# Fused attention, convolution and experts: counts summed in PSUM, the last tile in halves, three instead of five convolution units on TensorE, and new order tables

## The chip, the cores and the metric

The kernel runs on one core of a Trainium2 chip. Its time is device microseconds (us) per execution. Engines are named as in the profile: PE is TensorE's matmul side and PEld its weight loads, DVE is VectorE, ACT is ScalarE, POOL is GpSimd, and SP is SyncE, which here issues most DMAs. Lnnn is a line of the kernel before.

## What is computed

Attention on 8 batches of 8 heads, 256 tokens, 64 columns a head; a gated depthwise convolution of 15 taps over the tokens; and a mixture of 16 experts in which every token goes to one expert. All data are float32.

```python
attn = softmax(q @ k.T / 8)                       # per batch and head
x = (attn @ v)  -> (batch, token, 512)
xg = x * sigmoid(glu_gate)
conv[s, d] = sum_k pad(xg)[s + k, d] * conv_w[d, k]   # 15 taps, 7 zeros at each end
x = x + silu(conv)                                # 2048 tokens of 512 columns
g = argmax(x @ w_group);  e = argmax(x @ w_expert[g])
out = p(g) * p(e) * (relu(x @ w1[g, e]) @ w2[g, e])   # w1 512x1024, w2 1024x512
```

## The kernel before

**Tiling.** Work is cut into 16 units. A unit is one block of 128 channels (two heads) of two batches; four units, one for each channel block, make a group, so that group g holds batches 2g and 2g+1. Tiles lie with channels on the partitions and tokens along the free dimension, so most instructions work on 128x512 elements (two batches of 256 tokens).

**A unit.** `pair` (L472) makes the scores of two heads (L490), `head` takes their maximum on DVE (L519), the exponentials on ACT (L524) and transposes them on PE (L531); the transposes go back to SBUF as `pT`, and the product with v is L510. `tail` (L545) spreads the reciprocal sums into `rb`, transposes them on PE (L568), copies them out of PSUM (L570), multiplies (L577 to L582) and makes the gated `xg` (L586 to L593). A site such as `rb` or `xg` may run on one of two or three engines. Plain copies and casts go through one helper, and the trace shows them all at its line, L293.

**The convolution.** In `conv` (L640) DVE runs one multiply-add for each tap (L669, L671) into a PSUM bank. A few first taps may instead be made by ACT (L660) and added on POOL (L663). In `conv_pe` (L608) SP first copies `xg` four times, each partition in four shifted versions, into four weight buffers (L616); then PE multiplies them with small diagonal matrices, 16 matmuls of 32 rows by 512 columns (L626). Which units go this way stands in `PC`; 1 to 3 belong to group 0, and 4 and 5 to group 1. Then come tanh, the silu product (L636 or L691), the sum with x (L703), and the split of x into a rounded part `xh` and a rest `xl`.

**Routing.** Once four units of a group are done, `route` (L751) makes the logits on PE (L763), then a chain of small DVE instructions from L787 to L854 with three short visits to PE (L771, L819, L840/L841). For every batch of 256 tokens the expert that most of them chose is picked (L824, L826), and SP reads its number and fetches its weights (L860, L865). The place of every other token in its expert's list needs sums of one-hot counts over earlier tiles; `cum`, made by L836 and L838, is their running sum over the four tiles of a group.

**Experts.** A weight tile of 128x1024 arrives in `raw`, is rounded into `wh` (L884), and the rest is `wl` = raw - wh (L888, two halves). `dense` multiplies all 256 tokens of a batch with the chosen expert, three products for each pair of rounded and rest parts: 96 matmuls up (L914), then 48 of 512 columns down (L935 to L937) into two banks, one for each tile of 128 tokens. `store` (L966) scales a tile by the token's weight and sends it out. Tokens with another expert are gathered in lists of 32 (L1103 to L1201) and scattered over the result; a loop at the end takes what is left.

**The order.** Every engine runs its instructions in the order in which the program issues them. `Flow` makes that order while the program is built: each step has an engine, an assumed length and a key, and the ready step with the lowest key goes next. `KEYS` shifts the key of a site, `WAYS` picks the engine of each use of a site by a string of digits, `CD` delays the DVE convolution of a group behind other work, and `NSL`, `HB`, `NRAW`, `NPT` and `NPR` are numbers of buffers; `CSC`, `CS0`, `CAC` and `CMO` limit how many PSUM banks scores, convolutions and experts may hold. None of this runs on the chip: only the order and the choice of engines are left in the program.

Of the kernel before, what the change touches and what calls it, by code (L numbers as in the profile page):

```python
# [285 lines left out]
def attn_conv_moe(ctx, tc, aQ, aG, cw, wr, wE, cst, out):  # L286
# [185 lines left out]
    def pair(u, i):  # L472
# [13 lines left out]
        yield at("score", 0, u.k + 0.1 * i, ("PE", 0.875))  # L486
# [58 lines left out]
    def tail(u):  # L545
# [10 lines left out]
        e = yield at("rb", u.n, u.k, ("ACT", 0.1 + 0.21 * nb), ("DVE", 0.07 + 0.14 * nb), ("POOL", 0.5 * nb))  # L556
# [51 lines left out]
    def conv_pe(u):  # L608
# [4 lines left out]
        yield run("SP", 2.4, -20)  # L613
# [85 lines left out]
    def residual(u, acc, ia):  # L699
# [51 lines left out]
    def route(G_):  # L751
# [604 lines left out]
```

## Time and profile before

| | us |
|---|---|
| median of 3 runs | 369.69 |
| lowest and highest | 369.40, 369.95 |
| the profiled execution | 370.42 |
| its span, first to last instruction | 368.6 |
| PE busy | 348.4 (95% of the span) |
| DVE busy | 280.8 (76%) |
| POOL busy | 266.2 (72%) |
| ACT busy | 232.2 (63%) |

The span leaves out 1.8 us of the profiled execution. The shares are means over a kernel with several stages: attention with DMA and softmax in the first 100 us, attention beside experts until about 230 us, and experts alone after that. A matmul is drawn until its modelled end, so that rows of PE overlap; the time that PE needs for a run of matmuls is read from the start of its first to the start of what follows.

### The profile page before, as it was taken

Reading aid. Unit: us, or ns where it says so; the run is one execution under the profiler, and the core shown is the slowest. Engines: PE = TensorE matmul, PEld = TensorE weight load, DVE = VectorE, ACT = ScalarE, POOL = GpSimd, SP = SyncE. Lnnn points to the kernel's source line nnn. Section 1 sums busy time; section 2 is a strip of 40 time slices with the busy share of each in tenths; the row PEclk is TensorE's granted clock in tenths of the full one; section 3 lists DMA queues with packets and bytes.
Section 4 is the critical chain, followed back from the end, with each engine's and each line's share of the span. In section 5 each row is a group of like instructions: output and inputs, shape, how many; then the busy total and the mean of one; then the engine's idle time right before and its main releaser. Section 6 shows DMA issues by size and latency. Waiting matters only on the chain.

```text
span 368.6 us, 7954 instructions
## 1 busy us (share of the span) xinstructions
PE 348.4 (95%) x2766; PEld 277.0 (75%) x2766; DVE 280.8 (76%) x557; ACT 232.2 (63%) x534; POOL 266.2 (72%) x264
## 2 busy tenths in 40 slices
PE   7999999989999996998999999799999999999993
PEld 6666357635798776977787788779988977998982
DVE  3899948895999999999999999999999647201100
ACT  3987678746998653557989887344556534555521
POOL 1664766355887773569995866798869996999891
PEclk9999999999999998999999999899999999999999
DMA  7737964899266452549534332548999965855401
GB/s 269 246 117 177 305 225 150 198 322 325 97 238 218 166 195 77 203 132 339 217 115 172 116 114 88 199 136 288 412 409 390 371 249 186 307 195 181 163 2 64
DMA packets 29084, 77.13 MB, mean 209 GB/s; under 512 B 2999, under 2 KB 3255, under 8 KB 29041
## 3 DMA queue, kind: packets, MB, share of 16 engines
q1 hardware_dynamic: 27008, 72.94, 57.6%
q10 hardware_dynamic: 1872, 3.41, 2.5%
q8 instruction: 24, 0.39, 0.4%
q0 software_dynamic: 160, 0.23, 0.2%
q14 instruction: 20, 0.16, 0.1%
HBM read 63.67 MB, written 7.54 MB: 193 GB/s over the span
## 4 chain that ended last, share of the span: by engine, by line
PE 53%; DVE 25%; ACT 8%; DMA 6%; issue 4%; SPq 1%; POOL 1%; DVEq 0%; ACTq 0%; POOLq 0%
PE bk L914 19%; DVE bk L671 7%; PE bk L935 5%; PE bk L937 5%; PE bk L936 5%; ACT pr L524 5%; DVE nm L519 3%; PE bk L490 3%; PE bk L531 3%; PE bk L510 3%; DVE wl L888 3%; DMA gv<-wE 3%; PE bk L626 2%; DMA gv<-aG 2%; DMA wl<-sl 2%
## 5 line engine op out<-in xcount | busy, mean ns | idle before, releaser
L888 POOL TENSOR_TENSOR wl<-raw,wh 128x512 fp32r<-128x512 f32 x113 | 145.3, 1311 | 12.4 <-ACT wh L293 11.6
L671 DVE SCALAR_TENSOR_TENSOR bk<-sl,cwq,bk 128x512 f32<-128x512 f32 x143 | 102.6, 747 | 1.3
L914 PE MATMUL bk<-sl,wh 128*128 128x256 f32 x512 | 79.2, 294 | 0.0
L293 ACT CAST wh<-raw 128x1024 fp32r<-128x1024 f32 x57 | 60.1, 1054 | 23.9 <-PE bk L937 11.7
L914 PEld LDWEIGHTS bk<-sl,wh 128*128 128x128 f32 x512 | 68.5, 195 | 5.3 <-issue 3.9
L524 ACT ACTIVATE pr<-bk,nm 128x256 f32<-128x256 f32 x128 | 59.4, 493 | 19.4 <-DVE nm L519 18.9
L935 PE MATMUL bk<-wh,hh 128*128 128x512 f32 x128 | 51.8, 405 | 0.0
L936 PE MATMUL bk<-wl,hh 128*128 128x512 f32 x128 | 50.6, 395 | 0.0
L937 PE MATMUL bk<-wh,hl 128*128 128x512 f32 x128 | 50.6, 395 | 0.0
L519 DVE TENSOR_REDUCE nm<-bk 128x2 f32<-128x512 f32 x64 | 40.1, 681 | 8.3 <-PE bk L490 8.2
L961 POOL TENSOR_TENSOR hl<-tm,hh 128x512 fp32r<-128x512 f32 x20 | 27.0, 1352 | 19.8 <-ACT tm L954 14.8
L914 PE MATMUL bk<-sl,wl 128*128 128x256 f32 x256 | 41.4, 285 | 0.0
L531 PE MATMUL bk<-c_id,pr 128*128 128x128 f32 x256 | 36.2, 278 | 4.1 <-ACT pr L524 4.0
L948 ACT ACTIVATE hh<-bk 128x512 fp32r<-128x512 f32 x32 | 19.3, 603 | 31.7 <-PE bk L914 21.8
L531 PEld LDWEIGHTS bk<-c_id,pr 128*128 128x128 f32 x256 | 28.2, 140 | 13.1 <-ACT pr L524 8.3
L914 PEld LDWEIGHTS bk<-sl,wl 128*128 128x128 f32 x256 | 35.6, 193 | 0.0
L490 PE MATMUL bk<-qk 64*128 64x256 f32 x256 | 32.9, 392 | 0.1
L510 PE MATMUL bk<-pT,gv 128*64 128x256 f32 x256 | 32.7, 388 | 0.0
L490 PEld LDWEIGHTS bk<-qk 64*128 64x128 f32 x256 | 23.4, 186 | 7.4 <-issue 4.4
L524 ACT ACTIVATION_READ_ACCUMULATOR pr<-bk,nm 128x1 f32 x128 | 28.8, 225 | 0.0
L935 PEld LDWEIGHTS bk<-wh,hh 128*128 128x128 f32 x128 | 24.1, 188 | 5.9 <-issue 0.8
L937 PEld LDWEIGHTS bk<-wh,hl 128*128 128x128 f32 x128 | 24.1, 188 | 5.8
(161 smaller groups left out, 550.5 us busy)
## 6 DMA issues: line engine op xcount, KB each, us to landing
raw<-wE SPq DMA_DIRECT2D x64, 512.0 KB, 4.5
gv<-wE SPq DMA_DIRECT2D x24, 512.0 KB, 10.0
gv<-aG SPq DMA_DIRECT2D x16, 512.0 KB, 5.7
qk<-aQ SPq DMA_DIRECT2D x15, 512.0 KB, 3.7
wh<-sl SPq DMA_DIRECT2D x10, 270.0 KB, 6.1
wl<-sl SPq DMA_DIRECT2D x10, 270.0 KB, 5.7
out_dram<-y SPq DMA_DIRECT2D x9, 256.0 KB, 4.4
out_dram<-y ACTq DMA_DIRECT2D x7, 256.0 KB, 3.0
```

Source lines behind the costliest of these rows:

```text
L293: (a_.copy if e == "ACT" else on[e].tensor_copy)(o, i)
L490: t_.matmul(scs[hh][:, qt, :], t[sl, i, qt * P:(qt + 1) * P], t[sl, i, 256:512], start=True, stop=True)
L510: t_.matmul(u.a[64 * hh:64 * hh + 64, i, :], u.vt[:, i, kt, hh, :], pTs[hh][1][:, kt, :], start=kt == 0, stop=kt == 1)
L519: v_.reduce_max(nm[:, hh, :], sc, axis=AX.X, negate=True)
L524: a_.activation(pr[:, qt, :], sc[:, qt, :], AF.Exp, bias=nm[:, hh, qt:qt + 1], scale=1.0, accum_out=u.sm[:, i, qt, hh, 0:1])
L531: t_.transpose(tp[:, kt, qt * P:(qt + 1) * P], pr[:, qt, kt * P:(kt + 1) * P], ident)
L671: v_.scalar_tensor_tensor(acc if k == KT - 1 else ac, x, w, acc if k == m and m > 1 else ac, ALU.mult, ALU.add)
L888: on[e].tensor_tensor(wl[:, sl], raw[:, sl], wh[:, sl].bitcast(F32), ALU.subtract)
L914: t_.matmul(hp[:, f, :], ww[:, f, c, :], x, start=k == 0, stop=k == 11)
L935: t_.matmul(ys[t], hh[:, k, sl], w3h[:, k, :], start=j == 0 and k == 0, stop=False)
L936: t_.matmul(ys[t], hh[:, k, sl], w3l[:, k, :], start=False, stop=False)
L937: t_.matmul(ys[t], hl[:, k, sl], w3h[:, k, :], start=False, stop=j == 3 and k == 1)
```

## The change

Four things change.

1. The running sums of the one-hot counts are built in PSUM and copied to SBUF once, instead of being built in SBUF.
2. Of the last batch's second tile, the down product is made as two halves of 256 columns in two banks, each scaled and sent as soon as it is done (`half`), one by DVE and SP, one by ACT.
3. `PC` is 1 to 3: units 4 and 5 take the DVE convolution.
4. All tables are new, with the numbers of buffers, the limits of banks and some assumed lengths, so that sites move between engines and the order differs from about the tenth microsecond on.

```diff
-NSL = 22
-HB = 3
+NSL = 19
+HB = 4
-NRAW = 5
+NRAW = 6
-CD = 598.26, 74.86, 138.82, 696.08
+CD = 653.75, 89.0, 427.88, 891.21
-CSC = 6
-CS0 = 4
-CAC = 5
-CMO = 7
+CSC = 4
+CS0 = 5
+CAC = 3
+CMO = 4
-PC = 1, 2, 3, 4, 5
+PC = 1, 2, 3
...
         cum = small.tile([P, TT, NE], F32, name="cum")
-        v_.tensor_copy(cum[:, 0], ohl[:, 0])
+        sums = ps(0, TT, NE)
+        v_.tensor_copy(sums[:, 0], ohl[:, 0])
         for u in range(1, TT):
-            v_.tensor_tensor(cum[:, u], cum[:, u - 1], ohl[:, u], ALU.add)
-        yield run("PE", 0.5)
+            v_.tensor_tensor(sums[:, u], sums[:, u - 1], ohl[:, u], ALU.add)
+        v_.tensor_copy(cum, sums)
+        yield run("PE", 0.42)
...
-            iy = yield take("bk", 2, "mo", CMO + 2 * (att[0] == NU))
+            iy = yield take("bk", 3 if m.b == B - 1 else 2, "mo", CMO + 2 * (att[0] == NU))
...
+                    if m.b == B - 1 and t == 1:
...
+                        for h in range(2):
+                            yield run("PE", 0.71)
+                            c, yp = slice(h * S, h * S + S), ys[1 + h][:, 0:S]
+                            for k in range(2):
+                                t_.matmul(yp, hh[:, k, sl], w3h[:, k, c], start=j == 0 and k == 0, stop=False)
+                                t_.matmul(yp, hh[:, k, sl], w3l[:, k, c], start=False, stop=False)
+                                t_.matmul(yp, hl[:, k, sl], w3h[:, k, c], start=False, stop=j == 3 and k == 1)
+                            if j == 3:
+                                fl.go(half(m, h, c, y, yp), -5, fl.now[2], "PE")
+                        continue
...
+    def half(m, h, c, y, yp):
+        yield flag(gr[m.g].done)
+        tt = 2 * m.b + 1
+        yield run(("DVE", "ACT")[h], (0.35, 0.33)[h])
+        if h:
+            a_.activation(y[:, c], yp, AF.Copy, scale=rec[:, tt, 1:2])
+        else:
+            v_.tensor_scalar(y[:, c], yp, rec[:, tt, 1:2], None, ALU.mult)
+        w = ("SP", "ACT")[h]
+        yield run(w, 0.43)
+        on[w].dma_start(out=out[tt * P:(tt + 1) * P, c], in_=y[:, c])
```

What the tables make of the program, as numbers of instructions before and after. On DVE: multiply-adds of the convolution (L669, L671) 159 and 179; `wl` halves 15 and 2; copies of `rb` from PSUM 10 and 1; copies of `pT` 20 and 13; casts of `wh` 7 and 4; gated products L593 3 and 7; in all 586 and 580. On ACT: 434 and 462, among them taps of the convolution (L660) 6 and 16, `rb` from PSUM 6 and 15 and `pT` 44 and 51. On POOL: 280 and 290, among them `wl` halves 113 and 126, sums of taps (L663) 0 and 5, and `xg` products (L591) 13 and 9. On SP: copies for `conv_pe` (L616) 20 and 12.

On SP, before, just behind the first three weight fetches of group 0 (L865): `sl_632` is the `xg` of unit 5, `qk` and `gv` are the inputs of later units.

```order
49 L865 DMA raw<-wE 128x1024
50 L616 DMA wh<-sl_632 128x1x540
51 L616 DMA wl<-sl_632 128x1x540
52 L616 DMA wh<-sl_632 128x1x540
53 L616 DMA wl<-sl_632 128x1x540
54 L413 DMA qk<-aQ 128x2x512
55 L747 DMA x_rows<-y 128x512
56 L418 DMA gv<-aG 128x2x512
57 L865 ISA
58 L865 DMA raw<-wE 128x1024
```

The same place now (L867 is L865 of before):

```order
41 L867 DMA raw<-wE 128x1024
42 L413 DMA qk<-aQ 128x2x512
43 L418 DMA gv<-aG 128x2x512
44 L867 ISA
45 L867 DMA raw<-wE 128x1024
46 L867 ISA
47 L867 DMA raw<-wE 128x1024
48 L747 DMA x_rows<-y 128x512
49 L867 ISA
50 L867 DMA raw<-wE 128x1024
```

The four copies are gone, and the inputs of the next unit follow the first weight fetch.

On DVE, before, just ahead of the routing of group 0 (L787 is its first instruction): maxima, copies and a product.

```order
76 L293 COPY y<-bk_809 128x512
77 L593 SCALAR_TENSOR_TENSOR sl_503<-gv,sl_794 128x2x256
78 L554 TENSOR_REDUCE dn<-sm 128x8
79 L555 RECIPROCAL dn<-dn 128x8
80 L293 CAST sl_813<-sl_575 128x2x256
81 L714 TENSOR_TENSOR sl_884<-sl_575,sl_813 128x2x256
82 L293 COPY pT<-bk_800 128x512
83 L787 TENSOR_REDUCE gmx<-bk_809 128x4
```

The same place now, where `sl_553` is the `xg` of unit 4:

```order
73 L671 SCALAR_TENSOR_TENSOR bk_747<-sl_553,cwq,bk_747 128x512 x5
74 L636 SCALAR_TENSOR_TENSOR acc<-sl_441,bk_672 128x512
75 L671 SCALAR_TENSOR_TENSOR bk_747<-sl_553,cwq,bk_747 128x512 x2
76 L519 TENSOR_REDUCE nm<-bk_875 128x2
77 L519 TENSOR_REDUCE nm<-bk_876 128x2
78 L671 SCALAR_TENSOR_TENSOR bk_747<-sl_553,cwq,bk_747 128x512 x3
79 L671 SCALAR_TENSOR_TENSOR acc<-sl_553,cwq,bk_747 128x512
80 L787 TENSOR_REDUCE gmx<-bk_891 128x4
```

The convolution of unit 4, which PE did before, stands on DVE ahead of the routing of group 0.

On PE, before, at the routing of group 1: logits (L763), transposes of its rows (L741), and up products (L914) of the batches of group 0.

```order
509 L763 MATMUL bk_1767<-sl_1248,wr_sb 32x512
510 L741 MATMUL bk_1768<-c_id,sl_1248 128x128
511 L741 MATMUL bk_1768<-c_id,sl_1148 128x128
512 L741 MATMUL bk_1768<-c_id,sl_954 128x128
513 L741 MATMUL bk_1768<-c_id,sl_794 128x128
514 L771 MATMUL bk_1767<-c_sb,y 128x20 x4
515 L741 MATMUL bk_1769<-c_id,sl_1248 128x128
516 L741 MATMUL bk_1769<-c_id,sl_1148 128x128
517 L741 MATMUL bk_1769<-c_id,sl_954 128x128
518 L741 MATMUL bk_1769<-c_id,sl_794 128x128
519 L914 MATMUL bk_1839<-sl_727,wh 128x256
520 L914 MATMUL bk_1839<-sl_669,wh 128x256
```

The same place now (L951 to L953 are L935 to L937 of before):

```order
559 L763 MATMUL bk_1917<-sl_1240,wr_sb 32x512
560 L741 MATMUL bk_1919<-c_id,sl_1240 128x128
561 L741 MATMUL bk_1919<-c_id,sl_1124 128x128
562 L741 MATMUL bk_1919<-c_id,sl_935 128x128
563 L741 MATMUL bk_1919<-c_id,sl_698 128x128
564 L510 MATMUL bk_1940<-pT,gv 64x256 x4
565 L771 MATMUL bk_1917<-c_sb,y 128x20 x4
566 L741 MATMUL bk_1921<-c_id,sl_1240 128x128
567 L741 MATMUL bk_1921<-c_id,sl_1124 128x128
568 L741 MATMUL bk_1921<-c_id,sl_935 128x128
569 L741 MATMUL bk_1921<-c_id,sl_698 128x128
570 L510 MATMUL bk_1940<-pT,gv 64x256 x4
```

Between the short products of the routing PE now has attention and down products; 192 up matmuls stand ahead of this place, where 120 stood before.

## Rows read from the trace of the kernel before

**Rows 1.** The page: span, busy time by engine, shares of the last chain.
```profile
span 368.6 us, 7954 instructions
PE 348.4 (95%) x2766; PEld 277.0 (75%) x2766; DVE 280.8 (76%) x557; ACT 232.2 (63%) x534; POOL 266.2 (72%) x264
PE 53%; DVE 25%; ACT 8%; DMA 6%; issue 4%; SPq 1%; POOL 1%; DVEq 0%; ACTq 0%; POOLq 0%
```
**Rows 2.** Windows: stretch, length, busy by engine, clock, DMA share, GB/s.
```profile
50.00:100.00 50.00, 47.76 (x376) 29.82 (x374) 38.51 (x90) 37.13 (x107) 29.09 (x33) 1.00 0.67 214
100.00:134.90 34.90, 34.90 (x244) 28.76 (x240) 34.47 (x54) 27.14 (x64) 27.17 (x27) 1.00 0.59 211
134.90:231.00 96.10, 91.14 (x649) 76.23 (x648) 93.33 (x180) 68.93 (x164) 69.42 (x67) 0.98 0.46 156
296.70:368.60 71.90, 65.09 (x458) 56.91 (x448) 17.36 (x60) 30.21 (x41) 57.63 (x47) 0.99 0.47 162
```
**Rows 3.** Timeline of PE, 71 to 93 us: start, length, instruction, [idle before].
```profile
71.95 0.62 PE L626 MATMUL bk<-wh,wd 128*32 128x512 f32 x1
...
75.52 1.09 PE L531 MATMUL bk<-c_id,pr 128*128 128x128 f32 x8
...
80.65 1.04 PE L626 MATMUL bk<-wh,wd 128*32 128x512 f32 x2 [1.26 <-DMA wh<-sl]
...
86.98 2.00 PE L490 MATMUL bk<-qk 64*128 64x256 f32 x16
```
**Rows 4.** Timeline of the SP queue, 62 to 82 us.
```profile
76.38 1.68 SPq L616 DMA_DIRECT2D wl<-sl  x1
```
**Rows 5.** Groups by line and form: count | busy, mean ns | idle before.
```profile
L888 POOL TENSOR_TENSOR wl<-raw,wh 128x512 fp32r<-128x512 f32 x113 | 145.3, 1311 | 12.4 <-ACT wh L293 11.6 <-DVE wh L293 0.8
L888 DVE TENSOR_TENSOR wl<-raw,wh 128x512 fp32r<-128x512 f32 x15 | 15.8, 1083 | 0.5 <-ACT wh L293 0.3
L671 DVE SCALAR_TENSOR_TENSOR bk<-sl,cwq,bk 128x512 f32<-128x512 f32 x143 | 102.6, 747 | 1.3
L836 DVE COPY cum<-ohl_all 128x16 f32<-128x16 f32 x4 | 3.0, 754 | 0.1
L838 DVE TENSOR_TENSOR cum<-cum,ohl_all 128x16 f32<-128x16 f32 x12 | 6.2, 517 | 0.4
L845 DVE TENSOR_TENSOR base<-bk,base 128x16 f32<-128x16 f32 x4 | 0.7, 169 | 0.5 <-PE bk L841 0.5
L846 DVE TENSOR_TENSOR bk<-bk,base 128x64 f32<-128x64 f32 x4 | 0.9, 232 | 0.1
L593 DVE SCALAR_TENSOR_TENSOR sl<-gv,sl 128x512 f32<-128x512 f32 x3 | 3.2, 1081 | 0.1
L293 DVE COPY rb<-bk 128x512 f32<-128x512 f32 x10 | 6.8, 681 | 0.0
```
**Rows 6.** Waits, longest first: who for whom, us in total, times, longest.
```profile
PE bk L841 <- DVE cum L838: 2.2, 2, 1.9
```
**Rows 7.** Windows of DVE alone, around the routing of group 0.
```profile
0.00:64.30 64.30, 48.57 (x88) 1.00 0.67 213
64.30:134.90 70.60, 63.49 (x126) 1.00 0.67 222
```
**Rows 8.** Timeline of PE at the routing of group 1.
```profile
144.34 0.63 PE L819 MATMUL bk<-oh,c_sb 128*128 128x32 f32 x4 [2.79 <-DVE oh L813]
144.94 1.92 PE L914 MATMUL bk<-sl,wh 128*128 128x256 f32 x8
```
**Rows 9.** The chain that ended last: start, time on the chain, instruction.
```profile
24.54 1.06 PE bk L490 x8
47.25 1.93 PE bk L490 x16
317.16 11.26 PE bk L914 x96
362.19 0.69 ACT y L973
```

More of the change, by code (lines that the diff above doesn't have):

```diff
@@ L485, in pair @@
         nm = small.tile([P, 2, 2], F32, name="nm")
-        yield at("score", 0, u.k + 0.1 * i, ("PE", 0.875))
+        yield at("score", 0, u.k + 0.1 * i, ("PE", 0.87))
         for qt in range(2):
@@ L555, in tail @@
         v_.reciprocal(dn, dn)
-        e = yield at("rb", u.n, u.k, ("ACT", 0.1 + 0.21 * nb), ("DVE", 0.07 + 0.14 * nb), ("POOL", 0.5 * nb))
+        e = yield at("rb", u.n, u.k, ("ACT", 0.1 + 0.21 * nb), ("DVE", 0.07 + 0.14 * nb), ("POOL", 0.28 * nb))
         copy(e, rb[:, 0:nb].rearrange("p u (m d) -> p (u m) d", m=4),
@@ L612, in conv_pe @@
         ln = XW * (nb - 1) + S + KT - 3
-        yield run("SP", 2.4, -20)
+        yield run("SP", 4.3, -20)
         for j in range(4):
@@ L712, in residual @@
         u.xl = slot(u.nl, F32R, u)
-        e = yield at("xl", u.n, -3, ("POOL", 0.1 + 0.53 * nb), ("DVE", 0.1 + 0.27 * nb))
+        e = yield at("xl", u.n, -3, ("POOL", 0.1 + 0.57 * nb), ("DVE", 0.1 + 0.27 * nb))
         on[e].tensor_tensor(u.xl, x, u.xh.bitcast(F32), ALU.subtract)
@@ L768, in route @@
         lp, cp, rp = rt[:, 0:TT * 20], rt[:, 80:80 + nb * NE], rt[:, 112:112 + (TT + 1) * NE]
-        yield run("PE", 0.85)
+        yield run("PE", 0.82)
         for t in range(TT):
@@ L816, in route @@
         o4 = oh.rearrange("p (i t) e -> p t i e", i=nb)
-        yield run("PE", 0.5)
+        yield run("PE", 0.4)
         for t in range(2):
@@ L828, in route @@
         ohl = ohl_all[:, t0:t0 + TT, :]
-        yield run("DVE", 1.45)
+        yield run("DVE", 1.65)
         km = small.tile([P, nb], F32, name="km")
@@ L886, in split @@
             sl = slice(h * DM, h * DM + DM)
-            e = yield at("wl", 16 * m.b + 2 * n + h, -1, ("POOL", 1.24), ("DVE", 0.63))
+            e = yield at("wl", 16 * m.b + 2 * n + h, -1, ("POOL", 1.25), ("DVE", 0.63))
             on[e].tensor_tensor(wl[:, sl], raw[:, sl], wh[:, sl].bitcast(F32), ALU.subtract)
@@ L911, in dense @@
                             if k % UC == 0:
-                                yield run("PE", 0.12 * UC)
+                                yield run("PE", 0.1185 * UC)
                             x = (xs[c].xl if lo else xs[c].xh)[:, m.i, :]
@@ L931, in dense @@
                     sl = slice(t * P, (t + 1) * P)
+                    if m.b == B - 1 and t == 1:
+                        if j == 3:
+                            yield get("y")
+                            y = work.tile([P, DM], F32, name="y", bufs=2)
+                        for h in range(2):
[5 more added lines that the diff above has]
+                                t_.matmul(yp, hl[:, k, sl], w3h[:, k, c], start=False, stop=j == 3 and k == 1)
+                            if j == 3:
+                                fl.go(half(m, h, c, y, yp), -5, fl.now[2], "PE")
+                        continue
                     for k in range(2):
                         if DC or k == 0:
-                            yield run("PE", 0.71 if DC else 1.42)
+                            yield run("PE", 0.705 if DC else 1.41)
                         t_.matmul(ys[t], hh[:, k, sl], w3h[:, k, :], start=j == 0 and k == 0, stop=False)
@@ L970, in store @@
         tt = 2 * m.b + t
-        w = yield at("y", tt, -5, ("ACT", 0.55), ("DVE", 0.62))
+        w = yield at("y", tt, -5, ("ACT", 0.58), ("DVE", 0.65))
         if w == "ACT":
@@ L1104, in gather_all @@
                              io32.unsqueeze(1).broadcast_to([P, 4, m]), ALU.is_equal)
-            yield run("PE", 0.45)
+            yield run("PE", 0.62)
             for t in range(4):
@@ L1213, in first_tables @@
         n = yield take("bk", 1, "lo")
-        yield run("DVE", 5.1)
+        yield run("DVE", 5.5)
         tables_a(flat(bank(n)))
```

17 lines of the change are left out of this document (8 added, 9 removed).

## The prediction

> **What bounds the kernel now.** I read the page first, for the shares and the chain; then windows of 25 us and longer, for which engine is full where; then PE's own timeline for its gaps, and the groups by form for prices. PE is busy for 348.4 of 368.6 us, and the last chain runs on PE for 53% and on DVE for 25% [rows 1]. The windows say where. From 100 to 134.9 us PE and DVE are both full (34.90 and 34.47 of 34.90); from 134.9 to 231 DVE has 93.3 of 96.1 us and PE 91.1; after 296.7 DVE has 17.4 of 71.9 and PE 65.1 [rows 2]. So PE's work sets the end once the last group is routed, and before that DVE decides when a group can be routed. POOL and ACT have slack in the middle: POOL 96.6 of 131.0 us between 100 and 231, ACT 96.1 [rows 2].
>
> **The change part by part,** against the profiled execution, 370.42 us, which is 0.73 above the median of the runs.
>
> *(a) Two convolutions leave PE.* Unit 4 takes PE from 71.95 to 75.52, start to start, which is 3.57 us [rows 3]. Two of them: -7.1. PE has other work behind them (all the expert products wait in the order), so I count it in full.
>
> *(b) The waits at unit 5 go too.* PE stood 1.26 us for the shifted copies ahead of unit 5, and that unit took 6.33 us (80.65 to 86.98) instead of 3.57, 2.76 more for copies that had not landed: 4.0 together [rows 3]. In the same place SP issues the copies until 78.1 [rows 4], and the next `qk` and `gv` stand behind them in its order; now the inputs go ahead. What is late next there is the first expert product: its weights pass through ACT and POOL, and scores through DVE. Between 0 and -4.0 I take -3.0, nearer to the row, because SP and two of four weight buffers come free as well.
>
> *(c) Sums in PSUM.* A group's running sum costs DVE 754 + 3 x 517 = 2305 ns. In PSUM the nearest rows are 169 ns for 16 columns with one input in PSUM and 232 for 64: 4 x 169 + 232 = 908 ns [rows 5]. DVE saves 1.4 us a group, 5.6 in all. Where PE waited for it, that was 2.2 us in two waits [rows 6]. Between 0 and -2.2 I take -1.0, the middle: DVE's queue ahead of the sums may be late in their place.
>
> *(d) DVE's work moves forward.* Over the whole program DVE gets 20 more multiply-adds (20 x 747 = 14.9 us), and four gated products (4 x 1081 = 4.3); it loses 13 `wl` (13 x 1083 = 14.1), nine `rb` copies and seven `pT` copies (16 x 681 = 10.9) and the 5.6 of (c) [rows 5]. That is -11.4; with the smaller moves (casts and scalings away, sums and products to it) about -14. But up to the routing of group 1 the order has 28 more multiply-adds (20.9), and with the rest of that stretch (eight `rb` copies and six `wl` fewer, four maxima more, and so on) 9.5 us more work than before by the means, 11.8 if a `wl` half on DVE counts as an `rb` copy does. About half of it, the convolution of unit 4, stands ahead of the routing of group 0, where DVE has 15.7 us idle in 64.3; behind that, up to 134.9, it has 7.1 us idle in 70.6 [rows 7]. Those 7.1 can cover the other half, 5 to 6 us, though the first 15.7 lie partly where nothing is loaded yet. PE has cover as well: down and attention products now stand inside this routing, where PE stood 2.79 us before and then ran eight matmuls in 1.92 us [rows 8], and 72 more up matmuls stand ahead of it (0.117 us each, from 96 in 11.26 [rows 9]: 8.5 us). I take +2.5 for a later routing of group 1, between 0 (DVE has more ahead of it, so there is no gain) and +5.9 (nothing of the second half is covered). From there on DVE has some 24 us less to do than before, and is not the one that is late.
>
> *(e) More, smaller runs.* Runs of score and of attention products each rise by two, 19 to 21 and 23 to 25. A score run of 8 takes 1.06, one of 16 takes 1.93, so a cut costs 2 x 1.06 - 1.93 = 0.19 [rows 9]. Four cuts: +0.8, between 0 and +1.5.
>
> *(f) The last tile.* 24 matmuls become 48 of half the width. That changes nothing on PE if the time goes with the columns, as 0.117 for 256 columns suggests. The last scaling took 0.69 us [rows 9]; half a tile should take a little over half. I count -0.3, between +0.3 (if the cut costs as in (e)) and -0.7 (scaling hidden and a shorter last transfer).
>
> *(g) More on POOL and ACT.* POOL gets 13 `wl` (13 x 1311 = 17.0 us) and five sums, and loses four `xg` products and three copies: about +15, to 281. ACT gets 28 instructions of some 0.6 to 0.7 us, about +20, to 252. Both have room between 100 and 231, 34 us each, but a `wl` that is late holds PE, and `pT` and `rb` copies now queue behind rounding on ACT. Both loads only grow, so nothing is gained here. Between 0 and +5.0 (four `wl` halves that come too late, at 1311 ns each [rows 5]) I take +1.0, nearer to the slack.
>
> The rows of `wl` are worth weighing. POOL needs 1311 ns for one, DVE 1083 in the mean [rows 5]. The Trainium skill's page "GPSIMD Engine Reference", section "Performance versus the Vector engine", puts a two-input operation on POOL at about twice DVE's time and advises against such moves. By it DVE would save only 13 x 0.66 = 8.5 us (an estimate, half of POOL's time from the rows) for POOL's 17.0, and the move would be a loss where POOL is short. The page "SBUF — State Buffer", section "Who interferes with whom", explains the mean: a DVE instruction with two inputs in SBUF and a POOL instruction that reads SBUF exclude each other. By that, taking `wl` off DVE gives back the waiting too, and the row's 1083 is the price; the sum is made with the row.
>
> Sum: -7.1 - 3.0 - 1.0 + 2.5 + 0.8 - 0.3 + 1.0 = -7.1, so 363.3 for a profiled execution and **362.6 us** as a median.
>
> **The rivals.**
>
> *All of PE's work and waits come out.* PE is full and everything else is slack: (a), (b) and (c) in full, no late routing, nothing from POOL: -7.1 - 4.0 - 2.2 + 0.8 - 0.3 = -12.8, 356.9 as a median. For it: DVE's total falls by 14 us and its chain stretches lie between 100 and 231 [rows 2]. Against it: every other order of in-order queues brings waits of its own.
>
> *POOL becomes the bound.* The 17.0 us of `wl` lie mostly between 100 and 275. If a third of them, 5.7 us, stands in PE's way in place of (g)'s 1.0, the time is 367.3. For it: after 296.7 POOL already has 57.6 of 71.9 us and no `wl` there runs on DVE [rows 2], so it can build up no lead; the page on POOL named above speaks for this one. Against it: 34 us of room in the middle, and one more raw buffer.
>
> *Slower: the routing of group 1 waits for DVE.* All 11.8 us of added DVE work fall behind DVE's present end of that stretch, since its idle time lies where inputs were missing. PE then stands at L763, with everything of group 1 behind it, and nothing later gives that back. (d) is +11.8 instead of +2.5, and the slow run of matmuls after such a stand, 1.92 us instead of 0.94, adds 1.0 [rows 8, 9]: 362.6 + 10.3 = 372.9. It turns slower from a wait of 9.6 us on. For it: DVE was at 99% from 100 to 134.9 [rows 2]. Against it: unit 4's taps stand ahead of group 0's routing, and DVE's idle time of 7.1 us behind that.
>
> *It does little.* The waits only change places: (b) at 0, (g) at +5.0: 369.6.
>
> **How the numbers follow.** The forecast, with its own range of 359 to 366, has 0.60; all of PE's gain 0.14; POOL 0.14; slower 0.08; little 0.04. The range of 357.5 to 369.0 leaves out the last two and half of the second. About 0.2% (0.7 us) is what a measurement of this kernel can tell from no change. Faster: 0.60 + 0.14 + 0.14 = 0.88; same: 0.04; slower: 0.08.
>
> **What would show it.** (a), (b): no row of L626 after the routing of group 0, and no stand of PE above 1 us between that routing and the first up products. (c): the group of the prefix at 0.15 to 0.25 us an instruction, and no wait of PE for `cum` above 0.5 us. (d): PE's wait at the logits of group 1 under 3 us, and the last group routed at 284 to 291 instead of 296.7. (f): ACT's last scaling at about 0.4 us. (g): PE's waits for `wl` and for `pT` below 2 us in total. The forecast is wrong if PE's idle time in the middle grows by more than the two convolutions gave, wherever that is.

## The result and the profile after

| | before | after |
|---|---|---|
| median of the timed runs, us | 369.57 (4 runs, 369.40 to 369.95) | 358.41 (4 runs, 357.82 to 361.83) |
| ratio, 95% interval | | 0.9724, 0.9653 to 0.9795 |
| profiled execution, us | 370.42 | 361.83 |
| its span, us | 368.6 | 360.0 |
| logits of groups 0 to 3 (L763) start at | 59.3, 134.9, 219.4, 296.3 | 62.7, 142.8, 214.8, 280.0 |
| last matmul starts at, and from there to the end | 361.75, 6.9 | 352.28, 7.7 |

The kernel is 11.2 us faster; 7.1 were forecast. The profiled execution is 3.4 above its median, so that its traces show somewhat more loss than most executions have. The last group is routed 16.3 us earlier, but the stage behind it is 7.7 longer, because more products are left for it: 576 matmuls instead of 458 in the windows below and in [rows 2]. In the changed kernel L837 to L843 are the prefix and its products, L890 is `wl`, L916 the up and L951 to L953 the down products.

The page of the changed kernel (busy, chain; [rows 1] before):

```profile
PE 343.8 (96%) x2726; PEld 273.9 (76%) x2726; DVE 269.6 (75%) x551; ACT 247.9 (69%) x564; POOL 283.1 (79%) x274
...
PE 55%; DVE 17%; ACT 8%; DMA 6%; POOL 5%; issue 4%; SPq 1%; ACTq 0%; POOLq 0%; DVEq 0%
```

PE still bounds it. DVE has 17% of the chain instead of 25%, and POOL 5% instead of 1%. Windows, cut at the logits of groups 1, 2 and 3 ([rows 2] has 231.0 us for the second of these cuts, which is behind the logits at 219.4):

```profile
50.00:100.00 50.00, 46.46 (x317) 30.10 (x314) 42.56 (x96) 42.48 (x112) 29.68 (x34) 0.86 0.48 176
100.00:142.80 42.80, 42.80 (x313) 37.29 (x312) 40.95 (x64) 37.90 (x88) 32.95 (x35) 1.00 0.56 197
142.80:214.80 72.00, 70.81 (x495) 57.60 (x494) 68.99 (x132) 53.20 (x124) 65.44 (x60) 1.00 0.51 176
...
280.00:360.00 80.00, 71.19 (x576) 62.88 (x568) 15.55 (x61) 33.55 (x48) 64.95 (x53) 0.99 0.50 173
```

Between the logits of groups 1 and 2 PE is idle for 1.2 us. Before it was 4.8:

```profile
134.90:219.40 84.50, 79.72 (x554) 66.78 (x553) 82.49 (x148) 60.21 (x143) 61.25 (x59) 0.98 0.49 168
```

One window got worse: from 50 to 100 the clock is 0.86, where it was 1.00.

PE at the routing of group 1, [rows 8] before:

```profile
142.78 1.07 PE L763 MATMUL bk<-sl,wr_sb 128*32 128x512 f32 x8
...
144.36 1.08 PE L510 MATMUL bk<-pT,gv 128*64 128x256 f32 x8
...
151.21 0.53 PE L819 MATMUL bk<-oh,c_sb 128*128 128x32 f32 x4
```

The products of L819 come 8.4 us after the logits, before it was 9.4 (134.9 to 144.3), and PE does not wait: attention and down products fill the time. The prefix by form, [rows 5] before:

```profile
L839 DVE TENSOR_TENSOR bk<-bk,ohl_all 128x16 f32<-128x16 f32 x12 | 2.2, 182 | 0.4
...
L840 DVE COPY cum<-bk 128x64 f32<-128x64 f32 x4 | 0.9, 224 | 0.1
...
L837 DVE COPY bk<-ohl_all 128x16 f32<-128x16 f32 x4 | 0.7, 178 | 0.1
```

178 + 3 x 182 + 224 = 948 ns a group; the forecast had 908. The new loss is in PE's timeline from 75 us on:

```profile
76.98 0.66 PE L531 MATMUL bk<-c_id,pr 128*128 128x128 f32 x4 [1.23 <-ACT pr L524]
77.89 2.03 PE L531 MATMUL bk<-c_id,pr 128*128 128x128 f32 x8 [0.25 <-ACT pr L524]
79.85 3.17 PE L490 MATMUL bk<-qk 64*128 64x256 f32 x10
84.65 2.07 PE L490 MATMUL bk<-qk 64*128 64x256 f32 x6 [1.63 <-ACT pT L293]
...
87.70 3.68 PE L510 MATMUL bk<-pT,gv 128*64 128x256 f32 x16
```

PE waits for ACT, and what follows takes about twice its time: eight transposes 2.03 instead of 1.04, sixteen products 3.68 instead of 1.95. The windows show the granted clock at 0.50, which is 1.2 of 2.4 GHz:

```profile
78.00:84.00 6.00, 5.02 (x18) 3.00 (x18) 5.40 (x10) 3.48 (x8) 4.32 (x3) 0.50 0.99 359
84.00:90.00 6.00, 5.35 (x22) 3.22 (x24) 2.80 (x4) 5.75 (x14) 3.41 (x3) 0.50 1.04 404
```

ACT meanwhile stood for weights, ahead of the copy of `pT` that the scores need:

```profile
83.07 1.04 ACT L293 CAST wh<-raw 128x1024 fp32r<-128x1024 f32 x1 [2.18 <-DMA raw<-wE]
84.02 0.58 ACT L293 COPY pT<-bk 128x512 f32<-128x512 f32 x1
```

The loads of this stage now come together. SP issues six weight tiles, `qk` and `gv` between 73.5 and 79.0 us, where three of the six weight tiles were issued at 81.9 before. The DMA engines (the column before the last) are at 0.99 and 1.04 in the two windows above, after a stretch in which they had little to do:

```profile
50.00:76.00 26.00, 25.32 (x200) 16.03 (x196) 24.71 (x62) 23.49 (x66) 12.55 (x17) 1.00 0.33 123
```

Before, they were at 0.68 in that stretch and at 0.89 from 76 to 92 us. That this crowding makes the weights late fits these numbers, but no run tests it.

### The profile page after: what moved, and what is told of

It is laid out like the page before. It is cut to its first block, busy times and chain, and to the rows that moved or that the text cites. A ratio compares the mean times of both kernels' runs of the same rounds, so it can differ in the third digit from the quotient of the medians.

```text
span 360.0 us, 7864 instructions
## 1 busy us (share of the span) xinstructions
PE 343.8 (96%) x2726; PEld 273.9 (76%) x2726; DVE 269.6 (75%) x551; ACT 247.9 (69%) x564; POOL 283.1 (79%) x274
## 4 chain that ended last, share of the span: by engine, by line
PE 55%; DVE 17%; ACT 8%; DMA 6%; POOL 5%; issue 4%; SPq 1%; ACTq 0%; POOLq 0%; DVEq 0%
PE bk L916 18%; DVE bk L671 6%; PE bk L510 5%; PE bk L490 5%; PE bk L951 4%; POOL wl L890 4%; PE bk L531 4%; PE bk L952 4%; PE bk L953 4%; ACT pr L524 3%; DMA raw<-wE 2%; DVE nm L519 2%; DMA qk<-aQ 2%; PE bk L1220 2%; PE bk L1197 2%
## 5 line engine op out<-in xcount | busy, mean ns | idle before, releaser
L890 POOL TENSOR_TENSOR wl<-raw,wh 128x512 fp32r<-128x512 f32 x126 | 164.7, 1336 | 9.4 <-ACT wh L293 4.2
L671 DVE SCALAR_TENSOR_TENSOR bk<-sl,cwq,bk 128x512 f32<-128x512 f32 x161 | 114.5, 749 | 3.4 <-POOL sl L580 1.3
L293 ACT CAST wh<-raw 128x1024 fp32r<-128x1024 f32 x60 | 63.4, 1057 | 26.8 <-PE bk L953 19.4
L916 PE MATMUL bk<-sl,wh 128*128 128x256 f32 x512 | 76.4, 287 | 0.0
L916 PEld LDWEIGHTS bk<-sl,wh 128*128 128x128 f32 x512 | 66.1, 189 | 4.4 <-issue 3.7
L951 PE MATMUL bk<-wh,hh 128*128 128x512 f32 x120 | 49.3, 411 | 0.0
L952 PE MATMUL bk<-wl,hh 128*128 128x512 f32 x120 | 47.7, 398 | 1.4 <-POOL wl L890 1.4
L953 PE MATMUL bk<-wh,hl 128*128 128x512 f32 x120 | 47.5, 396 | 0.0
L916 PE MATMUL bk<-sl,wl 128*128 128x256 f32 x256 | 40.7, 281 | 0.0
L490 PE MATMUL bk<-qk 64*128 64x256 f32 x256 | 37.4, 417 | 1.7 <-ACT pT L293 1.6
L973 DVE SCALAR_TENSOR_TENSOR hl<-bk,hh 128x512 fp32r<-128x512 f32 x12 | 8.2, 686 | 36.0 <-ACT hh L964 36.0
L916 PEld LDWEIGHTS bk<-sl,wl 128*128 128x128 f32 x256 | 34.8, 188 | 0.0
L293 ACT COPY pT<-bk 128x512 f32<-128x512 f32 x51 | 29.4, 636 | 4.4 <-PE bk L531 4.0
```

Of the source, the lines that this page charges most:

```text
L293: (a_.copy if e == "ACT" else on[e].tensor_copy)(o, i)
L490: t_.matmul(scs[hh][:, qt, :], t[sl, i, qt * P:(qt + 1) * P], t[sl, i, 256:512], start=True, stop=True)
L671: v_.scalar_tensor_tensor(acc if k == KT - 1 else ac, x, w, acc if k == m and m > 1 else ac, ALU.mult, ALU.add)
L890: on[e].tensor_tensor(wl[:, sl], raw[:, sl], wh[:, sl].bitcast(F32), ALU.subtract)
L916: t_.matmul(hp[:, f, :], ww[:, f, c, :], x, start=k == 0, stop=k == 11)
L951: t_.matmul(ys[t], hh[:, k, sl], w3h[:, k, :], start=j == 0 and k == 0, stop=False)
```

## The experiments

Times of one batch share their runs of the kernel before: 369.15 (b_psum, b_unload, b_pc3, b_lean), 369.87 (a_sbuf, a_swap, a_whole, a_early), 369.38 (b_twice, a_warm, a_wl) and 369.26 (b_both). The ratios are against these runs, also for names in a_. Names in b_ start from the kernel before, those in a_ from the changed one, whose 358.41 is of another batch, so that a difference of 1 us from it says little.

**b_psum: the prefix alone, in the kernel before.**

```diff
-        v_.tensor_copy(cum[:, 0], ohl[:, 0])
+        sums = ps(0, TT, NE)
+        v_.tensor_copy(sums[:, 0], ohl[:, 0])
...
-            v_.tensor_tensor(cum[:, u], cum[:, u - 1], ohl[:, u], ALU.add)
+            v_.tensor_tensor(sums[:, u], sums[:, u - 1], ohl[:, u], ALU.add)
+        v_.tensor_copy(cum, sums)
```

> The kernel before with the prefix of counts made in PSUM and copied, in the same order of instructions (one more on DVE a group). Forecast (c): an instruction of it takes 0.15 to 0.25 us, a group's prefix 0.9 instead of 2.3 us, PE's two waits for cum (2.2 us) shrink below 0.5 in total, and the time falls by 1.0 (368.6), between 0 and 2.2. Rival 1 (PE then meets the half clock or a late bank just behind, and the waits change place): no change, 369.6 within 0.4. Rival 2 (the stretch of half clock behind the wait, 1.5 us at 233, goes with the wait): down by 2.5 to 4, 365.6 to 367.1.

Measured: 365.16 (363.54 to 366.23), ratio 0.9891 (0.9844 to 0.9939): -4.0, as rival 2 had it. PE at the prefix of group 2, before:

```profile
232.71 0.44 PE L841 MATMUL bk<-cum,c_sb 128*128 128x64 f32 x2 [1.89 <-DVE cum L838]
...
238.10 0.40 PE L935 MATMUL bk<-wh,hh 128*128 128x512 f32 x1
```

and in b_psum:

```profile
229.44 0.38 PE L842 MATMUL bk<-ohl_all,c_sb 128*128 128x64 f32 x2
229.66 0.39 PE L843 MATMUL bk<-cum,c_sb 128*128 128x64 f32 x2
...
233.49 0.40 PE L937 MATMUL bk<-wh,hh 128*128 128x512 f32 x1
```

From the prefix's second product (L841, now L843) to the first down product it was 5.39 us and is 3.83: the same 30 up products are 1.56 shorter, beside the wait of 1.89. A window of before shows the clock behind the wait:

```profile
234.00:236.00 2.00, 2.00 (x12) 2.00 (x11) 1.69 (x11) 1.96 (x3) 0.89 (x1) 0.50 0.93 299
```

DVE's timeline shows the prefix itself, the three sums before and then in b_psum:

```profile
230.02 2.63 DVE L838 TENSOR_TENSOR cum<-cum,ohl_all 128x16 f32<-128x16 f32 x3
```

```profile
228.46 0.61 DVE L839 TENSOR_TENSOR bk<-bk,ohl_all 128x16 f32<-128x16 f32 x3
```

Here a sum took 877 ns, not the mean of 517 [rows 5], while POOL was busy for all of 230 to 232. In PSUM it takes 203, again with POOL busy. PSUM is not faster in itself: at the routing of group 0 POOL was idle, and the three sums in SBUF took no longer than in PSUM. The twelve sums of the kernel before (shortest, median and longest in ns) show the same:

```profile
70.33 0.59 DVE L838 TENSOR_TENSOR cum<-cum,ohl_all 128x16 f32<-128x16 f32 x3
```

```profile
L838 DVE TENSOR_TENSOR cum<-cum,ohl_all x12: 174/176/1212, 70.3 to 308.0; 128x16 f32<-128x16 f32 x12
```

So the mean of 517 is made of sums of 174 to 176 and of a few that stood beside POOL. The Trainium skill's page "SBUF — State Buffer", section "Who interferes with whom", says that a DVE instruction with two SBUF inputs contends with a POOL instruction that reads SBUF, and that one with at most one SBUF input does not, outside the two-port modes, which a copy can enter. The rows agree: the sums do as told above, and the copy into `cum` (L836), with one SBUF input, took 0.18 us with POOL idle (a_sbuf, group 0) and 0.40 to 1.28 beside POOL.

**a_sbuf: the prefix back in SBUF, in the changed kernel.** The same edit the other way.

> The changed kernel with the prefix of counts made in SBUF again, in the same order. By the forecast's (c) DVE needs 1.4 us more for each of four groups. Theory (in the changed kernel PE has other work at the prefix, so DVE's 1.4 us is covered): up by 0 to 1, 358.4 to 359.4, and a wait of PE for cum below 1 us in total. Rival (each group's prefix stands on PE's way, and a half clock follows it): up by 2.5 to 5, 361 to 363.4.

Measured: 365.54 (364.55 to 365.63), 0.9872 (0.9827 to 0.9917): 7.1 above the changed kernel by the medians, 3.7 by the two profiled executions. The rival was right in direction; its range ended at 363.4. The 3.7 is too little, because the changed kernel's profiled execution had lost more ahead of this: a_sbuf is 2.5 us ahead of it at the logits of group 1 (140.3 and 142.8) and has lost that lead by group 3. From the logits of group 1 to the end a_sbuf takes 6.2 us more. Both kernels route group 3 at 280.0 us; PE then, in a_sbuf:

```profile
295.22 0.43 PE L841 MATMUL bk<-cum,c_sb 128*128 128x64 f32 x2 [1.60 <-DVE cum L838]
295.59 3.46 PE L1218 MATMUL bk<-gv,hT 128*32 128x128 f32 x64
298.98 0.61 PE L949 MATMUL bk<-wh,hh 128*128 128x512 f32 x1
```

and in the changed kernel:

```profile
293.46 0.39 PE L843 MATMUL bk<-cum,c_sb 128*128 128x64 f32 x2
293.77 1.95 PE L1220 MATMUL bk<-gv,hT 128*32 128x128 f32 x64
295.66 0.50 PE L951 MATMUL bk<-wh,hh 128*128 128x512 f32 x1
```

One wait of 1.60 costs 3.32 us here, because 64 products behind it take 3.46 instead of 1.95. Not every such wait has a half clock behind it: at group 1 PE waits 1.29 for `cum` in a_sbuf, and the clock stays at 1.00 from 152 to 160.

**b_unload: only the choice of engines for `wl`, `rb` and `pT`, in the kernel before.**

```diff
+            e = ("POOL", "DVE")[new("wl", 16 * m.b + 2 * n + h)]
...
-        copy(e, rb[:, 0:nb], tp[:, 0:nb])
+        copy(("ACT", "DVE")[new("rc", u.n)], rb[:, 0:nb], tp[:, 0:nb])
...
-        copy(e, pT, tp)
+        copy(("ACT", "DVE")[new("pT", hn)], pT, tp)
```

> The kernel before with the changed kernel's choice of engine for the wl halves (13 fewer on DVE, 13 more on POOL) and for the copies of rb and of pT from PSUM (about 16 fewer on DVE, 16 more on ACT); convolutions, order of every step and all else as before. It takes some 25 us off DVE and puts 17 on POOL and 9 on ACT. Theory (DVE being late costs PE its waits between 130 and 235 us, 2.9 at the routing of group 1, 2.1 at the prefix of group 2 and the half clock behind each, 1.5): down by 4 to 7, 362.6 to 365.6. Rival 1 (the forecast's (g): wl late on POOL and pT late on ACT give it back): 368.5 to 372. Rival 2 (PE's waits there are not due to DVE's load): 369.6 within 1.

Measured: 368.74 (367.37 to 369.94), 0.9991 (0.9946 to 1.0036): no change, which lies in the ranges of both rivals. By the trace rival 2 is wrong: the wait did hang on DVE's load, and it moved along DVE's chain. PE at group 1 (L827 is L819 of before, L849 is L841, L923 is L914):

```profile
143.40 0.53 PE L827 MATMUL bk<-oh,c_sb 128*128 128x32 f32 x4
...
149.39 0.43 PE L849 MATMUL bk<-cum,c_sb 128*128 128x64 f32 x2 [1.68 <-DVE cum L846]
...
151.04 1.91 PE L923 MATMUL bk<-sl,wh 128*128 128x256 f32 x8
```

The 2.79 us for `oh` are gone, 1.68 for `cum` stand in their place, and the slow products behind it as well. Something of rival 1's kind shows too: the logits of group 1 come 2.0 us later than before, at 136.95, and from 90 us to there PE waits 1.4 for `pr` of ACT and `rb` of POOL, where it was 0.2.

**b_both: b_psum and b_unload together.**

> The kernel before with both edits together: the prefix of counts in PSUM, and the changed kernel's choice of engine for wl, rb and pT; five units stay on TensorE, and the order of every step is kept. Alone the first gave -4.0 and the second -0.4: with the second, PE's 2.8 us for oh (L819) at the routing of group 1 went, and 1.7 us for cum (L841) came in its place, with a half clock behind it as before. Theory (one wait behind DVE had only moved along DVE's chain; with the prefix short as well it goes, with the half clock behind it, and so does the prefix of group 2): no wait of PE for oh or cum above 0.5 us, clock 1.00 from 140 to 155 and from 230 to 240, and 7 to 8.5 us below before: 360.9 to 362.4. Rival (the gains add up, and what is left waits elsewhere): -4.4, 365 within 1.

Measured: 365.20 (363.41 to 366.42, 5 runs), 0.9876 (0.9844 to 0.9908): -4.1, the rival. The waits and the half clock did go as the theory said (windows of PE, clock in the column before the last two):

```profile
135.00:150.00 15.00, 14.86 (x127) 13.65 (x126) 14.06 (x45) 8.92 (x16) 15.00 (x16) 1.00 0.57 208
150.00:155.00 5.00, 5.00 (x24) 4.01 (x23) 4.83 (x7) 2.25 (x4) 5.00 (x5) 1.00 0.94 274
155.00:219.00 64.00, 62.09 (x435) 50.48 (x434) 59.27 (x90) 54.24 (x136) 52.96 (x50) 1.00 0.50 166
```

The first down product of group 1's routing comes at 149.9 (b_psum 153.4), but logits of group 3 at 291.1 (b_psum 291.5). So the lead of 3.6 us over b_psum shrinks to 0.4. At the logits of group 1 b_both was 1.2 behind b_psum (136.5 and 135.3), at those of group 2 it is 1.3 ahead. PE is idle for 1.9 us from 155 to 219, and its waits for `pr` of ACT are 5.2 us in all, 4.0 before. ACT, which got the copies, seems to be what is late next; where the rest went is not settled.

**b_pc3: three units on TensorE, with the old tables.**

```diff
-CD = 598.26, 74.86, 138.82, 696.08
+CD = 598.26, 89.0, 138.82, 696.08
-PC = 1, 2, 3, 4, 5
+PC = 1, 2, 3
```

> The kernel before with PC of 1 to 3, so that units 4 and 5 take the DVE convolution, and one delay changed with it (the second of CD, 74.86 to 89.0), because the planner finds no order otherwise; the other tables stay, and the planner makes a new order. PE loses 7.1 us of work and the waits at unit 5, DVE gets 30 multiply-adds, 22 us, and no relief. Theory (DVE is full between 100 and 231 us, so that the two convolutions can leave PE only if DVE is unloaded elsewhere): PE's waits at the routing of groups 1 and 2 grow by 5 us or more, and the time is 368 to 376. Rival (the forecast's (a) and (b) come from PC alone, -7.1 and -3.0, whatever the tables): 359.5 to 363.

Measured: 412.19 (411.09 to 413.32), 1.117 (1.1124 to 1.1215): 43 us slower, far outside both. Windows:

```profile
100.00:150.00 50.00, 42.15 (x244) 32.45 (x243) 49.47 (x72) 26.72 (x59) 33.09 (x31) 0.83 0.37 124
150.00:200.00 50.00, 36.23 (x197) 29.41 (x196) 48.48 (x95) 21.85 (x45) 29.48 (x24) 0.80 0.43 149
```

DVE is full, PE has 21.6 of 100 us idle and a clock of 0.8. In the whole run PE waits 17.3 us for ACT's exponentials, which wait 26.6 for DVE's maxima, and 8.0 for `oh`. The planner's order is another one too, so the 43 us are not the price of `PC` alone; what they show is that with the old tables, and the order that comes of them, the two convolutions gain nothing. That room on DVE is what was missing fits the waits, but no run separates it from the order.

**b_twice: the convolution of units 4 and 5 twice.** For the first of a unit's four steps, five matmuls instead of one:

```diff
+                for k in ([0, 1, 2, 3, g] if u.n > 3 and g == 0 else [g]):
```

> The kernel before, where TensorE makes the 16 convolution matmuls of unit 4 and of unit 5 twice, the second set over the first; the order of all else is kept and so is the result. It adds to PE, at the place where the change takes it away, the work that (a) counts: 2 x 3.57 = 7.1 us. Theory (PE's work ahead of group 1's routing sets the end in full): 369.5 + 7.1 = 376.6, between 375.5 and 377.5. Rival (DVE, full from 100 to 231 us, is as late as PE there, so a part is covered): 371 to 374, with PE's 2.94 us at the routing of group 1 shrunk by what is covered.

Measured: 389.35 (388.93 to 389.56), 1.0548 (1.0495 to 1.0601): +20.0, not 7.1. The edit added more work than the expectation counted, as PE's timeline shows:

```profile
71.34 3.19 PE L627 MATMUL bk<-wh,wd 128*32 128x512 f32 x7
...
86.14 1.09 PE L531 MATMUL bk<-c_id,pr 128*128 128x128 f32 x8
```

Unit 4 takes 14.80 us, 11.23 more; unit 5 takes 14.80 as well (89.49 to 104.29), 8.47 more, less the 1.26 of its wait, which went. That is 18.4 of added work. At the end of unit 5 PE is 17.3 us behind the kernel before (104.29 and 86.98), and at the logits of group 1 16.7 (134.9 before):

```profile
151.63 1.06 PE L764 MATMUL bk<-sl,wr_sb 128*32 128x512 f32 x8
```

At those of group 2 it is 16.7 as well. So work of PE ahead of group 1's routing counts nearly in full up to there, while PE's wait for `oh` stayed at 2.8 (DVE moved back with it). The span grew by 18.8, but not by this alone: group 3 is 15.6 later, and the last stage is 3.2 longer, with a clock of 0.95 instead of 0.99.

**a_wl: the `wl` halves as before, in the changed kernel.**

```diff
+            e = ("POOL", "DVE")[old("wl", 16 * m.b + 2 * n + h)]
```

> The changed kernel with the engine of each wl half as the kernel before had it, in the changed kernel's order: 13 more of 128 run on DVE (some 0.94 to 1.08 us each, 12 to 14 us) and 13 fewer on POOL. Theory (between the routing of group 1 and of group 3 DVE, with 130 of 137 us, sets the time as PE does, so the tables had to take this work off it): PE's waits behind DVE in that stretch grow by 3 to 6 us and the time to 361 to 365. Rival 1 (the forecast's (g): POOL's wl are what PE waits for, 1.4 us in the last stage, so fewer on POOL help): 357 to 358. Rival 2 (neither, both are covered): 358.4 within 0.8.

Measured: 366.49 (364.31 to 368.49, 10 runs), 0.9927 (0.9895 to 0.9959): +8.1 by the medians, more than the theory, and +4.2 by the two profiled executions. PE's waits behind DVE come to 4.2 us, where the changed kernel has 0.2; the two longest (L771 is L763; the first is for a bank that DVE empties):

```profile
130.17 1.22 PE L925 MATMUL bk<-sl,wh 128*128 128x256 f32 x8 [1.01 <-DVE y L1012]
...
144.08 1.04 PE L771 MATMUL bk<-sl,wr_sb 128*32 128x512 f32 x2 [1.19 <-DVE sl L711]
```

**a_swap: one copy of `pT` ahead of the first cast on ACT.**

```diff
-        copy(e, wh, raw)
+        late.append((e, wh, raw)) if m.b == 0 and n == 1 else copy(e, wh, raw)
...
-        fl.back("bk", ns, "sc")
+        fl.back("bk", ns, "sc"); late and e == "ACT" and copy(*late.pop())
```

> The changed kernel with one pair of ACT's instructions exchanged: the copy of pT out of PSUM ahead of the first cast of wh, which in the profiled run stood 2.18 us for its weights at 80.9 us; nothing else moves. Theory (the only large stand of PE in the changed kernel, 3.2 + 1.6 us around 76 to 85 us and the half clock until 91, hangs on this wait of ACT, and the differences between runs of the changed kernel too, 357.5 to 362.5): 354 to 357.5, with all runs within 1.5 us. Rival 1 (PE's stand comes from the weights themselves or from DVE's maxima, so that it lasts as long): 358.4 within 1. Rival 2 (the runs of the changed kernel that took 357.8 did not have this stand at all, and the exchange only takes away the slow ones): 357.5 to 358.

Measured: 357.10 (356.61 to 359.33), 0.9668 (0.9614 to 0.9722). PE's wait of 1.63 is gone and group 3 is routed at 274.9, but the median is only 1.3 below the changed kernel's, within its spread: not told apart. Nor can the earlier routing be put down to the exchange alone. ACT's stand for these weights, 2.18 us in the changed kernel's profile, is 0.99 in a_whole and 1.17 in a_wl, which leave this place as it is; PE's wait behind it is 0.45 and 1.57 there, and a_whole routes group 3 at 276.7.

**a_warm: a_swap, and 14 matmuls of zeros where PE stood.**

```diff
+            for _ in range(n):
+                t_.matmul(wp[:, 0:WC], wz[:, 0:P], wz, start=True, stop=True)
```

> The changed kernel with the exchange of a_swap, and 14 matmuls of 128 zero columns on TensorE, into a free bank, just ahead of the transposes at which PE stood 1.23 us for ACT at 77.0 us. They compute nothing that is used. In a_swap the granted clock is half from 78 to 84.7 us; sixteen score matmuls take 4.87 instead of 2.00 us there and eight transposes 2.03 instead of 1.04. Theory (the stand at 76 us brings the half clock): the granted clock stays at 1.00 from 76 to 85, the scores take 2.0 to 2.3, and the time falls by 2.5 to 4 from a_swap's 357.1, to 353 to 354.6. Rival 1 (ACT's exponentials and copies are what is late there, and PE would only wait for them at full clock): 356.5 to 357.5. Rival 2 (the added matmuls are work in PE's way): 357.5 to 359.

Measured: 358.64 (357.49 to 360.10), 0.973 (0.9678 to 0.9783): no gain. The number lies in the range of rival 2 and is not told apart from a_swap's; the trace shows what rival 1 said.

```profile
75.88 0.94 PE L888 MATMUL bk<-wz 128*128 128x128 bf16 x14 [0.27 <-ACT rb L293]
...
80.80 3.68 PE L490 MATMUL bk<-qk 64*128 64x256 f32 x14 [0.85 <-ACT pT L293]
```

The clock stayed at 1.00 until 80 us (0.50 from 78 in a_swap). PE was then early, waited 0.85 for ACT, and the half clock came behind that. So with PE at full clock it is ACT that PE waits for there.

**a_whole: the last tile in one piece.**

```diff
-                    if m.b == B - 1 and t == 1:
+                    if False:
```

> The changed kernel with the last tile made as before, in one bank of 512 columns, scaled and sent in one piece. Forecast (f): up by 0.3, between -0.3 and +0.7. Theory from the changed kernel's trace (both halves are scaled by 352.6 us but their transfers wait until 353.7 for a scatter that POOL makes at 351.45): no change, 358.4 within 0.5. Rival (the end is the scaling and its transfer, so the halves gave 0.3 to 0.7): up by 0.3 to 0.7, with the last scaling at 0.6 to 0.7 us.

Measured: 359.30 (357.82 to 360.37), 0.9715 (0.9661 to 0.9769): within the spread. In the changed kernel the halves are scaled by 353.1, and their transfers wait for POOL's scatter, which starts 2.2 us ahead of them (2.3 in a_whole):

```profile
352.59 0.47 ACT L987 ACTIVATE y<-bk,rec 128x256 f32<-128x256 f32 x1 [0.68 <-PE bk L944]
353.68 0.36 ACTq L992 DMA_DIRECT2D out_dram<-y  x1
```

```profile
351.45 0.97 POOL L1229 DMA_INDIRECT out_dram<-ys,ixs  x1 [1.41 <-DMA out_dram<-ys,ixs]
```

**a_early: that scatter sooner.** `fl.go(spread(o), -50, fl.now[2])` instead of 50, and a new order from the planner.

> The changed kernel with the scatter of leftover tokens (L1229) ahead of the wl halves in POOL's order instead of behind them (its key is -50 instead of 50); the planner makes the order. Theory (the last stores wait for the last scatter, and 7.7 us pass from PE's last matmul to the end): the last scatter is done before PE's last matmul, the end comes some 1.4 us sooner, 357.0, between 356.5 and 358. Rival (the scatter delays wl halves on POOL, which leads the last stage, and PE waits 1.0 to 1.3 us more at each): 358.4 to 361.

Measured: 365.72 (363.66 to 367.77), 0.9879 (0.9813 to 0.9945): the rival, and worse than it. The last stage takes 86.7 us instead of 80.0. Each scatter but the first waits for the transfer of the one ahead of it, 3.22 and 1.41 us, and POOL's `wl` stand behind them:

```profile
317.09 0.97 PE L916 MATMUL bk<-sl,wl 128*128 128x256 f32 x4 [2.74 <-POOL wl L890]
```

A second wait for `wl` of 2.02 follows at 322.0, and the clock from 313 to 325 is 0.68. The order is a new one, so the loss is not shown to be the scatter's alone.

**b_lean: fewer convolution matmuls.** It was meant to take work off PE.

> The kernel before, where units 4 and 5 make only their first 4 of 16 convolution matmuls on TensorE; their shifted copies and everything else stay, in the same order. It leaves out 12 taps of these two units. That takes 2 x 12/16 x 3.57 = 5.4 us of work off PE. Theory (PE's work ahead of it sets the end, so that (a) counts in full): 369.6 - 5.4 = 364.2, within 1 us. Rival (DVE decides when groups can be routed between 100 and 231 us, and PE only waits longer there): 368.5 or more, with PE's wait at the logits of group 1 grown by 2 us or more.

Measured: 430.42, and it says nothing on (a): without those taps other tokens go to other experts, and PE has 3268 instructions instead of 2766, among them 256 more for the tokens outside the chosen expert (L1169 and L1192, 320 each instead of 192). b_twice took its place.

## Why the prediction was right, and where it was not

The direction held, and so did the range of 357.5 to 369.0. The forecast's own range, 359 to 366, did not: the median is 4.2 below 362.6, and the first rival's 356.9, which my range left out, was nearer, though not for its reasons. That the sum came within 4.2 is in part luck, since (b) erred one way and (c) and (d) the other. The term that was mis-sized and measured by itself is (c).

- **(a)** -7.1 is supported: b_twice has PE's work in that place counting nearly in full, 16.7 of 17.3 us. That taking it away pays as much in the new order was not measured by itself.
- **(b)** The 4.0 us at unit 5 went, as forecast, but the allowance for "what is late next" was too small. ACT is late for the scores of the next unit, and a half clock follows. My sign, no stand above 1 us ahead of the first up products, failed with 1.23 and 1.63. From 50 to 100 us PE is idle for 3.5 us instead of 2.2, and a mean clock of 0.86 over 50 us is 14 us at half speed, at most 7 lost, so that this stage gave up some 8 in the profiled execution (an estimate). The first up product comes at 91.3, before at 92.4. For this execution my -3.0 failed in the sign; the median execution is 3.4 shorter, and how much of that lies here was not measured. a_swap and a_warm shorten this stand without a clear gain.
- **(c)** -1.0, between 0 and -2.2, failed in size: -4.0 alone in the kernel before, and 3.7 to 7.1 in the changed one (6.2 by the traces from the routing of group 1 on). I took PE's waits as the whole price and halved them. The trace of before had the rest, the clock of 0.50 behind the wait, 1.5 us. I also read the mean of 517 ns as the price of a sum; a sum takes 174 to 176 beside an idle POOL, much as in PSUM (182), and the ones that PE waited for took 877.
- **(d)** +2.5 failed on the good side. The routing of group 1 is 7.9 us later, but PE had work until then and through it, and the 2.79 with its slow products (1.92 for 0.94 us of work [rows 8, 9]) went. The slower rival has its mechanism from here, and the tables kept it out: with 13 `wl` halves back on DVE (a_wl) PE stands at the logits of group 1, as that rival had it, and 4.2 to 8.1 us are lost. The rival's turning point of 9.6 us leaves out the 1.0 that it adds itself; with it, it is 8.6. That the last group is routed at 280.0, below my 284 to 291, is not a gain of that size, since the last stage is longer.
- **(e)** was not measured by itself. **(f)** can't be told from nothing, by a_whole: the tail waits for the scatter and takes 7.7 us instead of 6.9, and 7.5 in a_whole.
- **(g)** PE's waits for `wl` and `pT` come to 3.0, above the 2 I set:

```profile
PE bk L490 <- ACT pT L293: 1.6, 1, 1.6
PE bk L952 <- POOL wl L890: 1.4, 2, 0.7
```

The 13 halves on POOL are a gain here: with them on DVE the kernel is 8.1 slower by the medians. The Trainium skill's page "GPSIMD Engine Reference", section "Performance versus the Vector engine", advises against such moves. By the trace POOL takes 1.4 times as long for a half (1335 ns and 928 on DVE, in a_wl), but DVE was the engine that was late.

For the profiled execution an account by these terms is: -7.1 (a), -4.0 and +8 (b), -3.7 (c), -4.3 for the stand at group 1 with the half clock behind it (2.8 + 1.5), +0.8 (e), +0.8 tail; -9.5 in all, or -8.1 with the 1.4 that PE waits for `wl`, where the span fell by 8.6. It is an estimate: (e) is the forecast's own number, (a) and (c) come from runs in other orders, and no run has the new tables with five units on TensorE, so that (a), (b) and (d) are not separated. The terms don't add over kernels: the prefix is worth 4.0 in one order and 3.7 to 7.1 in the other, and b_both is no better than b_psum, though each of its two edits took a wait away.

## What to carry to other kernels

Price a wait of TensorE with what runs behind it: look at the granted clock in the two or three windows after the stand, and add the loss if there is one. Where a chain of small steps on one engine feeds another, take the duration at the place that is waited for and not the mean, see whether the same step is short elsewhere, and after removing one wait look at the next link of the same chain. A table of orders and a change of work are best tried as one edit: b_pc3, with a part of it, was 43 us slower than neither.

## What the runs showed that was not expected

- Two stands of 1.60 and 1.89 us on PE were followed by half the clock, and cost 3.3 and 3.6 us. This is counted from the prefix's first product to the next down product: 5.69 us in a_sbuf and 2.37 in the changed kernel, at group 3; 7.61 before and 4.05 in b_psum, at group 2. Stands of 1.29 (a_sbuf) and of 1.01 and 1.19 (a_wl) had a clock of 1.00 behind them.
- Three sums of 128x16 with both inputs in SBUF took 0.59 us while POOL was idle and 1.63 to 3.67 (a_sbuf at 291 us) while POOL was busy; with the running sum in PSUM they took 0.61 to 0.62 either way.
- Convolution matmuls with 32 output rows ran at 3.57 us for 16 when successive ones went to different groups of 32 rows, and a unit of 32 took 14.80 when five in a row went to the same group.
- A weight tile issued at 75.1 us behind other loads landed at 83.0, 7.9 us later; the median of the changed kernel's weight tiles is 6.0.
